# The last product of a gated attention and feed-forward kernel: scratch banks of two pieces, the order of the last two pieces, and a join of all columns

## The chip, the cores and the metric

The kernel runs on one core of a Trainium2 chip. The core has a matrix engine (TensorE, "PE" in the profile, with its weight loads as "PEld"), a vector engine (VectorE, "DVE"), a scalar engine (ScalarE, "ACT"), GpSimd ("POOL"), and a queue engine (SyncE, "SP") that here issues DMA transfers. Matrix products are accumulated in eight banks of 128 x 512 fp32 values, which DVE and ACT read. The metric is the device time of one execution in microseconds; less is better.

## The reference, cut to what matters

```
x = A_x                                    # 2048 rows, 1024 columns, bf16
g = sigmoid((x * gate_w).sum(-1))          # one number per row
a = attention(x, wqkv) @ wo                # 32 heads, 8 keys per query, 2 rows apart
h = gelu(x @ w_gate) * (x @ w_up)          # 3584 columns   (computed from B_x)
b = h @ w_down
return g * a + (1 - g) * b
```

The tail of the kernel, which this case is about, computes the two products with `wo` and `w_down` as one: the attention's output and h stand side by side as one long left operand, and `wo` and `w_down` one above the other as the right operand. The scale of the rows is applied when a finished sum leaves the banks.

## The kernel before, in words

The 2048 rows are cut into four chunks of 512. Most products are done by a scheme of the Strassen kind: two by two blocks, seven products instead of eight, with sums and differences of blocks ("forms") built by DVE. For the final product of a chunk (`down`, line 1635, and `down_rest`, line 1684) a block of 128 rows meets 18 tiles of 128 along the sum and 512 output columns. The seven products m = 0 to 6 each run for two pairs of row blocks, g = 0 and g = 1. In the last chunk product m = 5 is not done plainly for each g. `fifth` (line 1521) does both at once, by a second, inner scheme of the same kind: its left blocks are A(g, i), with i the even or odd tiles along the sum, its right blocks raw(i, j), with j the left or right half of the 512 columns (`lo` and `hi`, 256 each). Its forms are made well ahead by `fifth_rights` (line 1483) and `fifth_lefts` (line 1499).

The inner scheme has seven pieces, `o1` to `o7`, in the order of the code o1, o5, o6, o2, o7, o3, o4. Each is nine matmuls of 128 x 128 weights and 256 columns (`prod`, line 1540, matmul at line 1544). Three banks hold them:

- X is a scratch bank, taken by `bank_take` (line 267; of the free banks it gives the one that its last user leaves first). o1, o6 and o7 accumulate in its `lo` half, one on top of the other, and o5 stands in its `hi` half.
- Dk[0] holds an earlier product for g = 0; o2 adds to its `lo` half and o3 to its `hi` half.
- Dk[1] holds the same for g = 1; o4 adds to its `lo` half.

Beside each bank there is a fp32 buffer u2[g] (128 x 512) with a scaled product of before. `add` (line 1550, instruction at line 1552) scales a half of X by a number per row and adds it to a half of u2[g]. The adds are called a (after o1), b (two of them, after o5, one for each g), d (after o6) and f (two of them, after o7). `out` (line 1557, instruction at line 1562) scales a half of Dk[g], adds the half of u2[g] and writes the final bf16 half row; `evac` (line 1689, issue at line 1692) then has SP issue the store of that half to DRAM. There are four such joins: out(0, lo), out(1, hi), out(0, hi), out(1, lo).

The order of instructions on each engine is fixed when the program is built. A planner (`Weave`, line 44) walks through streams of operations that carry estimated costs and dependencies, and emits the one that can start first; every engine then runs its list in order. The stream of `fifth` is one generator, so its own operations come in the order of its `yield`s. The dependencies handed to `pe` and `dve` guide the planner. The waits that really go into the program are set from what each instruction reads and writes, and the buffers it shares with others.

Two instructions near the tail that the steps also use: line 1715, a join of the same form as line 1562 over all 512 columns, used for another product of the same chunk; and line 1700, ACT's scaled copy of a whole bank.

Of the kernel before, what the change touches and what calls it, by code (L numbers as in the profile page):

```python
# [155 lines left out]
def kernel(  # L156
# [12 lines left out]
    nc = tc.nc  # L169
# [21 lines left out]
    NW = D // 2  # L191
# [39 lines left out]
    banks = [psum.tile([P, SC], F32, name=f"ps{i}") for i in range(8)]  # L231
# [3 lines left out]
    w = Weave(nc, tc)  # L235
# [18 lines left out]
    def dve(cost, fn, deps=(), **kw):  # L254
        return Op("DVE", cost, fn, deps, **kw)
# [4 lines left out]
    def pe(n, fn, deps=(), **kw):  # L260
        return Op("PE", n * MM, fn, deps, tail=0.17, **kw)
# [5 lines left out]
    def bank_take(seeded=False, dirty=False):  # L267
        ok = [i for i in range(len(bank_free)) if not (seeded and bank_free[i][0] in partly)]
        if dirty:
            ok = [i for i in ok if bank_free[i][0] in partly] or ok  # L270
        best = min(ok, key=lambda i: -1.0 if bank_free[i][1] is None else bank_free[i][1].end)
        partly.discard(bank_free[best][0])
        return bank_free.pop(best)
# [1181 lines left out]
    lefts = [hT[:, 0:KP, NST - 1, :], hT[:, KP:2 * KP, 0, :], hT[:, KP:2 * KP, 1, :]]  # L1455

    def wide(q, k):
        if q < 8:
            return flat_of(lend[q // 4])[:, (q % 4 * 4 + k) * HW:(q % 4 * 4 + k + 1) * HW]
        return hrow[:, 20 + k // 2, k % 2 * HW:(k % 2 + 1) * HW]  # L1460

    def raw5(q, i, j):
        if q < 8:
            return flat_of(lend[4 + q // 4])[:, (q % 4 * 4 + 2 * i + j) * HW:(q % 4 * 4 + 2 * i + j + 1) * HW]
        return hrow[:, 18 + i, j * HW:(j + 1) * HW]
# [13 lines left out]
    def halves(c):  # L1479

        return {(g, i): [z.rearrange("p (q i) s -> p q i s", i=2)[:, :, i] for z in views(c)[g]["S4"]] for g in range(2) for i in range(2)}
# [39 lines left out]
    def fifth(c, Dk, u2, ops, omg, evac, ost_tile):  # L1521
        RT = {1: 0, 3: 1, 2: 2, 4: 3}
        S = halves(c)
        nh = FH // 2
        X, fr = bank_take()
        lo, hi = slice(0, HW), slice(HW, 2 * HW)

        def A(g, i):
            return lambda q: S[g, i][0][:, q] if q < nh else S[g, i][1][:, q - nh]

        def of(z):
            return lambda q: z[:, q]

        def raw(i, j):
            return lambda q: raw5(q, i, j)

        def T(f):
            return lambda q: wide(q, RT[f])

        def prod(bk, cols, lhs, rhs, start, deps):  # L1540
            for q0 in range(0, KP, 3):
                def fn(q0=q0):
                    for q in range(q0, q0 + 3):
                        nc.tensor.matmul(banks[bk][:, cols], lhsT=lhs(q), rhs=rhs(q), start=(start and q == 0),  # L1544
                                         stop=(q == KP - 1), skip_group_check=True)
                o = pe(1.515, fn, [x_ for x_ in deps if x_ is not None])
                yield o
            return o

        def add(g, cols, src, deps):  # L1550
            om = omg[:, 2 * g:2 * g + 1]
            return dve(0.42, lambda: nc.vector.scalar_tensor_tensor(out=u2[g][:, cols], in0=banks[X][:, src], scalar=om, in1=u2[g][:, cols],
                                                                    op0=ALU.mult, op1=ALU.add), deps)

        boxes = [[], []]

        def out(g, cols, deps):
            om = omg[:, 2 * g:2 * g + 1]

            def fn():  # L1560
                dst = boxes[g][0] if boxes[g] else ost_tile(boxes[g])
                nc.vector.scalar_tensor_tensor(out=dst[:, cols], in0=banks[Dk[g]][:, cols], scalar=om, in1=u2[g][:, cols],  # L1562
                                               op0=ALU.mult, op1=ALU.add)
            yield from evac(dve(0.42, fn, deps), 2 * g, 1, boxes[g], cols.start, cols.stop)
        rights = [("ir5", q) for q in range(KP)]
        raws = [("fw", q) for q in (0, 4, 7, 8)]
        j = {n: [("j%d" % n, k) for k in range(2)] for n in (1, 2, 3, 4)}
        m5 = [("inner", c)]
        o1 = yield from prod(X, lo, A(0, 0), raw(0, 0), True, [fr] + raws + [("S4", c, 0, 1)])
        a = add(0, lo, lo, [o1])  # L1570
        yield a
        o5 = yield from prod(X, hi, of(lefts[0]), T(1), False, rights + j[1])
        b = [add(g, hi, hi, [o5]) for g in range(2)]
        yield from b
        o6 = yield from prod(X, lo, of(lefts[1]), T(2), False, [a] + j[2])
        d = add(0, hi, lo, [o6])
        yield d
        o2 = yield from prod(Dk[0], lo, A(0, 1), raw(1, 0), False, m5)
        yield from out(0, lo, [o2, a])
        o7 = yield from prod(X, lo, A(1, 0), T(3), False, [d] + j[3])  # L1580
        f = [add(1, cols, lo, [o7]) for cols in (lo, hi)]
        yield from f
        o3 = yield from prod(Dk[0], hi, of(lefts[2]), raw(1, 1), False, j[4])
        yield from out(1, hi, [f[1], b[1]])
        yield from out(0, hi, [o3, d, b[0]])
        o4 = yield from prod(Dk[1], lo, A(1, 1), T(4), False, [])
        yield from out(1, lo, [o4, f[0]])
        w.done["pr", c, 5, 1] = o4

    def views(c):  # L1590
        cc = c % 2
# [92 lines left out]
    def down_rest(c, prod, ops, ev, A, Bk, Dk, m5, u2, omg, steps):  # L1684
# [35 lines left out]
        for m, g in steps:  # L1720
            if True:
# [17 lines left out]
                elif m == 3:  # L1739
                    o = yield from prod(Bk[g], m, g, False, [ev[g, "seed"]])  # L1740

                    def cp2(g=g, om1=om1):
                        u2[g] = work.tile([P, NW], F32, tag="u2", bufs=2, name="u2d")
                        scaled(Bk[g], om1, u2[g][:])
                    ev[g, "u2"] = act(0.6, cp2, [o])
                    yield ev[g, "u2"]
                elif m == 4:
                    ev[g, "m4"] = yield from prod(Bk[g], m, g, False, [ev[g, "u2"]], hooks=hk4 if g else hk3)
                    if g or c < INNER:
                        yield from joined(g)  # L1750
                elif m == 5 and c >= INNER:
                    yield from fifth(c, Dk, u2, ops, omg, evac, ost_tile)
                elif m == 5:
                    o = yield from prod(Dk[g], m, g, False, [ev[g, "m5"]])
                    e = dve(0.67, lambda g=g, om1=om1, box=box: nc.vector.scalar_tensor_tensor(
                        out=ost_tile(box), in0=banks[Dk[g]][:], scalar=om1, in1=u2[g][:], op0=ALU.mult, op1=ALU.add),
                        [o, ev[g, "u2"]])
                    yield from evac(e, j1, 1, box)
                    bank_give(Dk[g], e)
                else:  # L1760
                    o = yield from prod(Bk[g], m, g, False, [ev[g, "x"]])
                    e = act(0.6, lambda g=g, om2=om2, box=box: scaled(Bk[g], om2, ost_tile(box)), [o])
                    yield from evac(e, j2, 0, box)
                    bank_give(Bk[g], e)
# [58 lines left out]
```

## Time and profile before

| what | value |
|---|---|
| median of 3 timed runs | 717.35 us (717.07 to 718.23) |
| the profiled execution, its own time | 716.05 us |
| its span (first to last recorded event) | 714.3 us |
| PE busy | 704.8 us, 99% |
| DVE busy | 645.8 us, 90% |
| ACT busy | 328.9 us, 46% |
| POOL busy | 73.8 us, 10% |
| mean granted clock of PE | 0.999 |
| the pieces of `fifth`, first matmul to last | 701.58 to 711.2 us |
| last DVE instruction (line 1562) | 711.24 to 711.72 us |

The profile is of one execution. A timeline row gives the start, the duration, the engine, the line of the kernel, output <- inputs and the number of instructions merged in it; in brackets stands how long the engine had been idle before, and which instruction released it. The ends of matmuls are modelled, so gaps between matmuls are also read from start to start. Within the tail, "ps" is a bank, "u2d" the buffer u2, "ost" an output row block, "omg" the numbers per row, and "lend", "hT", "qo" hold blocks and forms.

### The profile page before, as it was taken

What the parts mean: (1) busy time and instruction counts of PE and PEld (TensorE: products, weight loads), DVE (VectorE), ACT (ScalarE), POOL (GpSimd) and SP (SyncE); (2) the same over time, 40 slices, a digit from 0 to 9 for tenths busy, and PEclk for the clock granted to TensorE, in tenths of its full rate; (3) what the DMA queues carried; (4) which work ended last, traced back from release to release, by engine and by line L of the source; (5) the groups of instructions that cost most, each with busy time, mean ns of one, the idle gap of its engine ahead of it and who ended that gap; (6) DMA issues with size and microseconds to landing.
All of it is one profiled execution on the core that took longest, in us unless ns stands there. A gap on an engine that the chain in (4) does not pass through costs nothing. (4 is left out here: it accounts for less than half of the span.)

```text
span 714.3 us, 10025 instructions
## 1 busy us (share of the span) xinstructions
PE 704.8 (99%) x3310; PEld 348.9 (49%) x3375; DVE 645.8 (90%) x963; ACT 328.9 (46%) x557; POOL 73.8 (10%) x130
## 2 busy tenths in 40 slices
PE   9999999999999999999999999999999999999997
PEld 5566544444444444456664444444444444444464
DVE  4999999999999999999689999899899999859782
ACT  5454685555665522153465313357655764221110
POOL 0040133433211000100000000100000000001000
PEclk9999999999999999999999999999999999999999
DMA  9963799996997799944459899996846574999980
GB/s 267 375 242 100 224 264 330 365 337 207 223 278 230 241 248 345 347 151 147 113 148 339 271 311 349 314 289 203 242 134 177 152 211 129 325 325 360 398 309 30
DMA packets 183477, 179.47 MB, mean 251 GB/s; under 512 B 56321, under 2 KB 139009, under 8 KB 183169
## 3 DMA queue, kind: packets, MB, share of 16 engines
q1 hardware_dynamic: 173808, 148.15, 70.0%
q0 software_dynamic: 9328, 30.42, 11.5%
q8 instruction: 26, 0.43, 0.2%
q10 hardware_dynamic: 288, 0.26, 0.1%
q14 instruction: 27, 0.21, 0.1%
HBM read 135.27 MB, written 31.46 MB: 233 GB/s over the span
## 5 line engine op out<-in xcount | busy, mean ns | idle before, releaser
L1241 PEld LDWEIGHTS <-ring 128*128 128x128 bf16 x1568 | 153.4, 98 | 184.9
L1241 PE MATMUL ps<-lend,ring 128*128 128x512 bf16 x878 | 210.9, 379 | 0.9
L1241 PE MATMUL ps<-tf,ring 128*128 128x512 bf16 x659 | 162.9, 379 | 0.7
L1659 PE MATMUL ps<-ring,hT 128*128 128x512 bf16 x665 | 153.5, 379 | 0.8
L1659 PEld LDWEIGHTS <-hT 128*128 128x128 bf16 x680 | 66.5, 98 | 79.8
L844 PEld LDWEIGHTS <-ring 128*128 128x128 bf16 x512 | 64.9, 127 | 45.8 <-DVE tf L533 0.4
L1189 DVE TENSOR_TENSOR xbuf<-xbuf,lend 128x2048 bf16<-128x2048 bf16 x64 | 77.9, 1221 | 3.0 <-DMA xbuf<-xbuf 2.8
L1042 DVE TENSOR_TENSOR xbuf<-qo,lend 128x2048 bf16<-128x2048 bf16 x64 | 77.2, 1219 | 0.0
L1048 DVE TENSOR_TENSOR xbuf<-xbuf 128x2048 bf16<-128x2048 bf16 x56 | 68.3, 1220 | 0.2
L844 PE MATMUL ps<-tf,ring 128*128 128x512 bf16 x251 | 57.8, 379 | 0.2
L844 PE MATMUL ps<-lend,ring 128*128 128x512 bf16 x250 | 57.5, 379 | 0.4
L1317 ACT ACTIVATE gl<-ps 128x512 bf16<-128x512 f32 x56 | 33.4, 597 | 48.1 <-PE ps L1241 46.9
L1273 ACT COPY ps<-ps 128x512 f32<-128x512 f32 x56 | 32.1, 573 | 50.7 <-PE ps L1241 50.5
L1692 POOL DMA_DIRECT2D out_dram<-ost x24 | 13.0, 541 | 338.0 <-ACT ost L1700 251.0
L1659 PE MATMUL ps<-ring,qo 128*128 128x512 bf16 x180 | 46.9, 379 | 0.2
L1700 ACT ACTIVATE ost<-ps,omg 128x512 bf16<-128x512 f32 x16 | 11.0, 687 | 78.1 <-PE ps L1659 74.9
L521 POOL DMA_DIRECT2D fforms<-ring x56 | 30.6, 546 | 127.0 <-DVE ring L512 114.0
L1290 DVE TENSOR_TENSOR hT<-hT,gl 128x1024 bf16<-128x1024 bf16 x56 | 38.4, 686 | 5.6 <-ACT hT L1283 5.4
L1329 DVE TENSOR_TENSOR u<-ps,u 128x512 f32<-128x512 f32 x56 | 38.5, 688 | 3.3 <-PE ps L1241 2.5
L1308 DVE TENSOR_TENSOR hT<-ps,m 128x512 bf16<-128x512 f32 x56 | 38.5, 687 | 2.4 <-PE ps L1241 2.2
L1325 ACT COPY u<-ps 128x512 f32<-128x512 f32 x56 | 32.8, 585 | 15.5 <-PE ps L1241 15.5
L1199 DVE TENSOR_TENSOR xbuf<-xbuf 128x2048 bf16<-128x2048 bf16 x32 | 39.1, 1221 | 0.1
(166 smaller groups left out, 728.5 us busy)
## 6 DMA issues: line engine op xcount, KB each, us to landing
ring<-dforms SPq DMA_DIRECT2D x105, 256.0 KB, 5.4
ring<-in_B_w_down_dram SPq DMA_DIRECT2D x77, 256.0 KB, 5.3
ring<-in_B_w_gate_dram SPq DMA_DIRECT2D x56, 256.0 KB, 5.5
fforms<-ring POOLq DMA_DIRECT2D x56, 256.0 KB, 5.4
ring<-fforms SPq DMA_DIRECT2D x56, 256.0 KB, 4.5
ring<-in_B_w_up_dram SPq DMA_DIRECT2D x42, 256.0 KB, 5.2
ring<-in_A_wqkv_dram SPq DMA_DIRECT2D x32, 256.0 KB, 4.5
ring<-oforms SPq DMA_DIRECT2D x30, 256.0 KB, 5.6
```

Of the source, the lines that this page charges most:

```text
L844: nc.tensor.matmul(banks[bk][:], lhsT=lhsT, rhs=rhs[:, kt, :], start=(start and kt == 0), stop=(kt == KH - 1), skip_group_check=True)
L1042: V(out=w3(box[t]), in0=q_b, in1=k_w, op=ALU.mult)
L1048: V(out=w3(box[0]), in0=w3(box[0]), in1=w3(box[t]), op=ALU.add)
L1189: return dve(tt(n), taking(("p", t), lambda: V(out=w3(box["p", t]), in0=w3(box["ab"]), in1=v_w, op=ALU.mult)), [("qkv", c, 2, t), abo] + ( ...
L1199: V(out=p0.rearrange("p (u n) -> p u n", u=2), in0=lo, in1=hi, op=ALU.add)
L1241: nc.tensor.matmul(banks[bk][:], lhsT=wv[:, k, fl * P:(fl + 1) * P], rhs=rhs[:, k, :], start=(start and k == 0), stop=(k == KH - 1), skip_ ...
L1290: yield dve(tt(2 * SC), lambda hv=hv, gv=gv: nc.vector.tensor_tensor(out=hv, in0=hv, in1=gv, op=ALU.mult), [e, ev[f, "g1"], ev[f, "g2"]], ...
L1308: ev[f, "up2"] = dve(tt(SC, True), lambda f=f: nc.vector.tensor_tensor(out=hs(f, 1), in0=v3(banks[Bk[f]][:]), in1=v3(m5[f][:]), op=ALU.add ...
L1317: nc.scalar.activation(out=gl[f][:, r1 * SC:(r1 + 1) * SC], in_=banks[A[f]][:], func=ACT.Gelu_apprx_tanh)
L1325: nc.scalar.copy(out=u2[f][:], in_=banks[Bk[f]][:])
L1329: e = dve(tt(SC, True), lambda f=f: nc.vector.tensor_tensor(out=u2[f][:], in0=banks[Dk[f]][:], in1=u2[f][:], op=ALU.add), [o, ev[f, "u2"]])
L1659: nc.tensor.matmul(banks[bk][:, o0:o0 + cols[1] - cols[0]], lhsT=l, rhs=wv[:, i, cols[0]:cols[1]], start=(start and k == 0), stop=(q == la ...
```

## The change

A second scratch bank Y is taken beside X. The piece o5 goes to the `lo` half of Y, as the first product of that bank, and its two adds b read Y. The other scratch pieces stay in X. The two last pieces change places: o4 now comes directly behind o7 and its adds f, and o3 is last. The two joins for g = 1 become one of all 512 columns behind o4, with one store of 128 KB; the join and store for g = 0, `hi`, are last. There are as many matmuls as before, of the same shapes; one DVE instruction and one store fewer.

```diff
         X, fr = bank_take()
+        Y, fy = bank_take()
...
-        def add(g, cols, src, deps):
+        def add(g, cols, bk, deps):
...
-            return dve(0.42, ... in0=banks[X][:, src], scalar=om, in1=u2[g][:, cols],
+            return dve(0.42, ... in0=banks[bk][:, lo], scalar=om, in1=u2[g][:, cols],
...
-            yield from evac(dve(0.42, fn, deps), 2 * g, 1, boxes[g], cols.start, cols.stop)
+            yield from evac(dve(0.67 if cols.stop - cols.start == NW else 0.42, fn, deps), 2 * g, 1, boxes[g], cols.start, cols.stop)
...
         o1 = yield from prod(X, lo, A(0, 0), raw(0, 0), True, [fr] + raws + [("S4", c, 0, 1)])
-        a = add(0, lo, lo, [o1])
+        a = add(0, lo, X, [o1])
         yield a
-        o5 = yield from prod(X, hi, of(lefts[0]), T(1), False, rights + j[1])
-        b = [add(g, hi, hi, [o5]) for g in range(2)]
+        o5 = yield from prod(Y, lo, of(lefts[0]), T(1), True, [fy] + rights + j[1])
+        b = [add(g, hi, Y, [o5]) for g in range(2)]
         yield from b
         o6 = yield from prod(X, lo, of(lefts[1]), T(2), False, [a] + j[2])
-        d = add(0, hi, lo, [o6])
+        d = add(0, hi, X, [o6])
         yield d
         o2 = yield from prod(Dk[0], lo, A(0, 1), raw(1, 0), False, m5)
         yield from out(0, lo, [o2, a])
         o7 = yield from prod(X, lo, A(1, 0), T(3), False, [d] + j[3])
-        f = [add(1, cols, lo, [o7]) for cols in (lo, hi)]
+        f = [add(1, cols, X, [o7]) for cols in (lo, hi)]
         yield from f
+        o4 = yield from prod(Dk[1], lo, A(1, 1), T(4), False, m5)
+        yield from out(1, slice(0, NW), [o4, b[1]] + f)
         o3 = yield from prod(Dk[0], hi, of(lefts[2]), raw(1, 1), False, j[4])
-        yield from out(1, hi, [f[1], b[1]])
         yield from out(0, hi, [o3, d, b[0]])
-        o4 = yield from prod(Dk[1], lo, A(1, 1), T(4), False, [])
-        yield from out(1, lo, [o4, f[0]])
-        w.done["pr", c, 5, 1] = o4
+        w.done["pr", c, 5, 1] = o3
```

More of the change, by code (lines that the diff above doesn't have):

```diff
@@ L1548, in prod @@
             return o
-        def add(g, cols, src, deps):
+        def add(g, cols, bk, deps):
             om = omg[:, 2 * g:2 * g + 1]
-            return dve(0.42, lambda: nc.vector.scalar_tensor_tensor(out=u2[g][:, cols], in0=banks[X][:, src], scalar=om, in1=u2[g][:, cols],
+            return dve(0.42, lambda: nc.vector.scalar_tensor_tensor(out=u2[g][:, cols], in0=banks[bk][:, lo], scalar=om, in1=u2[g][:, cols],
                                                                     op0=ALU.mult, op1=ALU.add), deps)
```

## The prediction

> **What bounds the kernel now.** I read the page first: TensorE (PE) is busy 704.8 us of the 714.3 us span, the granted clock is 0.999, and the chain of waits that ended last runs only through PE and the VectorE (DVE) combines of the last product. The diff touches nothing but that product, so I went to the last 14 us. There the waits view, for 700 to 716 us (columns: total us, times, longest), shows PE waiting for DVE three times:
>
> ```profile
> DVE u2d L1552 <- PE ps L1544: 9.7, 4, 6.8
> ...
> PEld L1544 <- issue: 2.6, 3, 1.1
> PE ps L1544 <- DVE u2d L1552: 1.5, 2, 1.0
> ...
> PE ps L1544 <- DVE ost L1562: 0.6, 1, 0.6
> ```
>
> Three holes, 1.5 + 0.6 = 2.1 us by modelled matmul ends, 2.6 us by the weight loads beside them. The timeline view (start, duration, engine, line, what; in brackets the idle time before it and its releaser) places them:
>
> ```profile
> 702.46 0.27 PE L1544 MATMUL ps<-hT,qo 128*128 128x256 bf16 x1
> ...
> 702.77 0.48 DVE L1552 SCALAR_TENSOR_TENSOR u2d<-ps,omg,u2d 128x256 f32<-128x256 f32 x1 [6.76 <-PE ps L1544]
> 703.30 1.03 PE L1544 MATMUL ps<-lend,hT 128*128 128x256 bf16 x8 [0.57 <-DVE u2d L1552]
> ...
> 704.17 0.27 PE L1544 MATMUL ps<-hT 128*128 128x256 bf16 x1
> 704.48 0.88 DVE L1552 SCALAR_TENSOR_TENSOR u2d<-ps,omg,u2d 128x256 f32<-128x256 f32 x2 [1.24 <-PE ps L1544]
> 705.41 1.03 PE L1544 MATMUL ps<-lend,hT 128*128 128x256 bf16 x8 [0.97 <-DVE u2d L1552]
> ...
> 706.28 0.27 PE L1544 MATMUL ps<-hT 128*128 128x256 bf16 x1
> 706.39 0.93 PE L1544 MATMUL ps<-lend,hT 128*128 128x256 bf16 x7
> ...
> 709.23 0.27 PE L1544 MATMUL ps<-hT 128*128 128x256 bf16 x1
> 709.53 0.88 DVE L1562 SCALAR_TENSOR_TENSOR ost<-ps,omg,u2d 128x256 bf16<-128x256 f32 x2
> 710.06 0.92 PE L1544 MATMUL ps<-lend,hT 128*128 128x256 bf16 x7 [0.56 <-DVE ost L1562]
> ...
> 710.93 0.27 PE L1544 MATMUL ps<-hT,qo 128*128 128x256 bf16 x1
> 711.24 0.48 DVE L1562 SCALAR_TENSOR_TENSOR ost<-ps,omg,u2d 128x256 bf16<-128x256 f32 x1 [0.84 <-PE ps L1544]
> ```
>
> The reader should see a strict alternation at the three holes: PE ends a piece, DVE reads the bank, and only then PE goes on. The listed dependencies do not ask for it: o5 (the piece of line 1572) does not list the add a, o6 (1575) lists a and not the adds b, o4 (1586) lists nothing. Each waits because it writes the other half of a bank that DVE is just reading. Between holes PE starts a matmul each 0.11 us (706.28 to 706.39); a piece of nine takes 0.98 us.
>
> **The change, part by part.** I count holes from start to start, less the 0.11 us pitch.
>
> (1) *o5 gets the bank Y.* Now o5 starts at 703.30, after the add a (ends 703.25); it could start at 702.46 + 0.11 = 702.57. Gain 0.73 us. In the changed program's list of instructions the first matmul of o5 carries no wait; its ninth carries one on DVE, for a right-hand form that the timeline shows done at 696.0, or at the latest for a, over at 703.25 when that matmul is due at 703.44. Cost nothing either way.
>
> (2) *o6 no longer waits for b.* Now it starts at 705.41, with the last matmul of o5 at 704.17: 705.41 - 704.28 = 1.13 us gone. What is late next: o6 still needs a. On the new clock o5 starts at 702.57, o6 is due at 703.55, and a ends at 703.25 plus 0.05 us (703.25 to 703.30 now). Cover 0.25 us; without it the excess would be paid.
>
> (3) *o4 goes ahead of o3, with one join of 512 columns.* Now o4 starts at 710.06 where 709.23 + 0.11 = 709.34 was possible: 0.72 us gone. o4's bank was last read by ScalarE, in the copy that started at 692.29, so its wait is long satisfied. A satisfied wait costs nothing that shows: o2's first matmul carries one on ScalarE already and starts 0.11 us after its predecessor (706.39). o3 writes a bank that the join out(0, lo) has read; that join moves to about 705.7 to 706.2, and o3 is due at 707.48.
>
> Sum for PE: 0.73 + 1.13 + 0.72 = **2.58 us**. The last matmul starts at 710.93 - 2.58 = 708.35 instead of 710.93.
>
> (4) *Does DVE keep up?* On the new clock: a 702.77 to 703.25; both b 703.75 to 704.63; d at 704.73 (o6's last matmul at 704.42 plus the 0.31 us between 710.93 and 711.24) to 705.21, and o7 needs d at 705.52 (cover 0.26 us after the 0.05); out(0, lo) 705.71 to 706.19; both f 706.69 to 707.57; o4's last matmul starts at 707.37, so the join can start at 707.68. It is dearer than a half: the same form at 512 columns (line 1715) took 0.75 us against 0.48. It ends at 708.43, and out(0, hi) is due at 708.35 + 0.31 = 708.66. Cover 0.23 us. The join carries six semaphore waits; line 1715 with five ran after two queue events of 50 and 154 ns, so I bound the added event between 0 and 0.15 us. That fits under the cover, and I take 0. For all of DVE: 0, bounds 0 to 0.25 us, as if the cover were overdrawn by its own size. No bound below nothing: the last instruction is the same 256-column form.
>
> (5) *Stores.* SP issues two instead of three after the halves: 128 KB after the join (issue at 708.47), 64 KB after the last (709.18). An issue occupies SP 0.33 to 0.38 us, so the second finds the queue free. After an engine's end at 702.47 the 128 KB store moved its data from about 703.33 to 703.9; shifted to 708.43 that is 709.3 to 709.9, while the last store's data starts 0.85 us after its combine's end (712.55 after 711.72 now), at 710.0. They just miss each other. I take 0, bounds 0 and 0.5 us (the whole transfer of the 128 KB). From the last combine to the span's end I keep 714.3 - 711.72 = 2.58 us, which only by chance is the same number.
>
> The Trainium skill, *DMA: Bandwidth & Descriptors*, section "Queues, rings and completion order", speaks against this tail: a completion signal lands only after every earlier write of the same DMA engine, so a large store just ahead can hold back the small one. By that rule the last store could not complete before the 128 KB one; the landings of the trace, 1.7 us for 128 KB and 1.6 us for 64 KB, give 710.2 and 710.8, so the sum stays as it is by the rule too.
>
> **Sum.** The profiled execution took 716.05 us, span 714.3; minus 2.58 gives 713.47, span 711.7. The median of the timed runs is 717.35, 1.30 us above the profiled one; the holes are in both, so I forecast **714.8 us**, 0.36% less. A measurement of this kernel can tell about 0.2%, 1.43 us, from no change (the three runs span 1.16).
>
> **The rivals.**
>
> *The holes shrink but do not all go.* The covers are 0.23 to 0.26 us. If DVE starts later than I have it by twice the cover, at a, d and the join, that returns some 0.75 us; with the last transfer queued, 0.5 more. That gives up to 1.25 us back: 714.8 to 716.0. For it: the covers are thin against waits of 0.05 us. Against: they come from one regular rhythm, and d to o7 has the same cover now (d ends 707.07, o7 starts 707.38 without a hole).
>
> *Nothing gained: the end is a transfer.* The join's store could land late. It decides the end from a landing of 714.3 - 0.94 - 708.47 = 4.9 us (0.94 being what follows the last landing now, 711.76 + 1.6 to 714.3). The first store of this chunk, at 690.37, did take 5.0 us, with 383 GB/s of loads around it. That would give 717.4. Against: the load traffic is over by 695.0, and all later stores landed in 1.6 to 1.7 us. By the rule of the Trainium skill named above this case would hold the last store as well; it adds no time. The same 717.4 comes out if the change does not do what it says and a wait on DVE reappears at each piece; the list of waits speaks against that.
>
> *Slower: PE loses clock.* Without holes PE runs the 54 matmuls from o5 on in one go, 54 x 0.109 = 5.9 us at full clock. The windows view shows that this core does grant half a clock, in the idle tail (columns: stretch, length, busy times of PE, PEld, DVE, ACT and POOL, PEclk, DMA share, GB/s):
>
> ```profile
> 712.60:712.90 0.30, 0.00 (x0) 0.00 (x0) 0.00 (x0) 0.00 (x0) 0.00 (x0) 0.84 0.73 212
> 712.90:713.20 0.30, 0.00 (x0) 0.00 (x0) 0.00 (x0) 0.00 (x0) 0.00 (x0) 0.50 0.01 2
> ```
>
> If dense work drew the same answer, 5.9 x (1/c - 1) would eat the gain from a clock of c = 0.70 down; at 0.50 it costs 5.9 us, and 714.8 + 5.9 = 720.7. Against: that reduction follows idleness, and in the windows from 694 to 702 us, with PE busy throughout, the clock is 1.00.
>
> **How the numbers follow.** Forecast 0.80, at 714.8 with its own range 714.0 to 715.6. Shrunk holes 0.10, up to 716.0, about 0.07 of it still over 0.2%. Nothing gained 0.07. Slower 0.03. So faster 0.80 + 0.07 = 0.87, same 0.03 + 0.07 = 0.10, slower 0.03. The range goes up to 716.0 (the first rival and all bounds of (4) and (5), 0.75 us, and a spread of runs on them) and down to 713.8, since the profiled execution shows that a run can lie 1.30 us under the median; that leaves out the last two rivals and a little of the spread.
>
> **What would show it.** In the changed kernel's timeline: 63 matmuls of the last product at one pitch, about 701.6 to 708.6, no idle entry on PE above 0.1 us, at o5, o6 and o4 each; one 128x512 combine of 0.75 us that starts near 707.7; the last combine at about 708.7, directly behind PE; two landings of 1.6 to 1.7 us; span 711.7. Wrong would be an idle entry on PE with a DVE releaser (steps 1 to 3), a last combine that follows DVE rather than PE (4), or more than 2.7 us from the last combine to the end (5). If all of that holds and the time does not move by 2 us or more, then the time outside the span, or some earlier part, moved the other way, and my premise that nothing ahead of the last product changes is wrong.

## The result and the profile after

| | before | after |
|---|---|---|
| timed runs, median | 717.07 us (715.95 to 718.23, 7 runs) | 714.59 us (713.38 to 715.37, 7 runs) |
| profiled execution, its own time | 716.05 us | 713.38 us |
| its span | 714.3 us | 711.6 us |
| first matmul of the last product to the end of the span ("the tail") | 701.58 to 714.3: 12.72 us | 701.42 to 711.6: 10.18 us |

The changed kernel is faster by 0.35%: ratio 0.9965, 95% interval 0.9952 to 0.9978, by the medians 2.48 us. The forecast was 714.8. Of the 2.7 us between the two spans, 2.54 us lie in the tail and 0.16 us in its earlier start.

The waits view of the changed kernel for 700 to 716 us (total us, times, longest) has three rows, of which two concern the last product:

```profile
DVE u2d L1553 <- PE ps L1545: 7.8, 3, 6.8
...
DVE ost L1563 <- PE ps L1545: 0.7, 2, 0.5
```

The reader is to see what is missing: no row in which PE waits for DVE is left, and the row of held-up weight loads (2.6 us) is gone too. In both rows that are left it is DVE that waits for PE. The timeline at the places of the three holes (start, duration, engine, line, what, idle time before and its releaser; the lines of the kernel moved down by one):

```profile
701.42 0.93 PE L1545 MATMUL ps<-lend,hT 128*128 128x256 bf16 x7
...
702.29 0.27 PE L1545 MATMUL ps<-hT,qo 128*128 128x256 bf16 x1
...
702.40 1.04 PE L1545 MATMUL ps<-lend,hT 128*128 128x256 bf16 x8
702.61 0.48 DVE L1553 SCALAR_TENSOR_TENSOR u2d<-ps,omg,u2d 128x256 f32<-128x256 f32 x1 [6.76 <-PE ps L1545]
703.28 0.27 PE L1545 MATMUL ps<-hT 128*128 128x256 bf16 x1
703.39 1.04 PE L1545 MATMUL ps<-lend,hT 128*128 128x256 bf16 x8
703.59 1.47 DVE L1553 SCALAR_TENSOR_TENSOR u2d<-ps,omg,u2d 128x256 f32<-128x256 f32 x3 [0.50 <-PE ps L1545]
...
706.22 0.27 PE L1545 MATMUL ps<-hT,qo 128*128 128x256 bf16 x1
...
706.33 0.93 PE L1545 MATMUL ps<-lend,hT 128*128 128x256 bf16 x7
...
707.21 0.27 PE L1545 MATMUL ps<-hT,qo 128*128 128x256 bf16 x1
...
707.32 1.04 PE L1545 MATMUL ps<-lend,hT 128*128 128x256 bf16 x8
707.60 0.75 DVE L1563 SCALAR_TENSOR_TENSOR ost<-ps,omg,u2d 128x512 bf16<-128x512 f32 x1 [0.19 <-PE ps L1545]
708.19 0.27 PE L1545 MATMUL ps<-hT 128*128 128x256 bf16 x1
708.50 0.48 DVE L1563 SCALAR_TENSOR_TENSOR ost<-ps,omg,u2d 128x256 bf16<-128x256 f32 x1
```

At 702.40 o5 starts 0.11 us behind o1 and runs beside the add a; at 703.39 o6 starts 0.11 us behind o5, beside b; at 706.33 o4 starts 0.11 us behind o7, beside the adds f; at 707.32 o3 starts 0.11 us behind o4, beside the wide join. The last combine starts at 708.50, 0.31 us behind the start of the last matmul, so PE and not DVE sets it.

### The profile page after: what moved, and what is told of

The parts are those of the page before. It is cut to its first block, busy times and chain, and to the rows that moved or that the text cites. A ratio compares the mean times of both kernels' runs of the same rounds, so it can differ in the third digit from the quotient of the medians.

```text
span 711.6 us, 10088 instructions
## 1 busy us (share of the span) xinstructions
PE 707.3 (99%) x3375; PEld 348.7 (49%) x3375; DVE 645.5 (91%) x962; ACT 329.1 (46%) x557; POOL 74.0 (10%) x130
## 4 chain that ended last, share of the span: by engine, by line
PE 97%; DMA 2%; SPq 0%; DVE 0%; issue 0%
PE ps L1241 48%; PE ps L1659 28%; PE ps L844 19%; DMA lend<-in_A_x_dram 1%; PE ps L613 1%; PE ps L1545 1%; PE ps L1412 1%; DMA hT<-in_A_x_dram 1%; SPq L442 0%; DVE tf L533 0%; PE ps L946 0%; DVE ost L1563 0%; PE ps L1003 0%
```

## The experiments

The theory: PE lost 2.58 us because three pieces write a bank that DVE is just reading, in other columns; each hole is 0.31 us (last matmul's start to DVE's start), plus the DVE work up to the end of its read of that bank, plus 0.05 us back to PE, less the pitch of 0.11 us, and less what PE does meanwhile. The main rival: the gain comes from the new order and the wide join, that is from one instruction and one store less. I judge by the tail, since its start alone differs by up to 2.9 us between the traces below (701.42 to 704.34). Spans are printed to 0.1 us, so a tail is known to about 0.05. The starts of the first and the last matmul of the last product are printed to 0.01 us, so the stretch between them shows the holes alone, without the stores; it has a column of its own. The two parts (bank only, order and join only) were timed in 11 runs each, the kernel before beside them in 21; each of the other variants ran once, and for them only the trace counts.

| kernel | tail starts | span | first to last matmul, us | tail, us | tail expected |
|---|---|---|---|---|---|
| before | 701.58 | 714.3 | 9.35 | 12.72 | |
| as changed | 701.42 | 711.6 | 6.77 | 10.18 | 10.14 (12.72 - 2.58) |
| bank only | 703.06 | 713.9 | 7.49 | 10.84 | 10.86 |
| order and join only | 703.12 | 715.2 | 8.63 | 12.08 | 12.00 |
| join in halves | 702.05 | 712.2 | 6.77 | 10.15 | 10.2 to 10.3 |
| half of the join ahead of o4 | 701.42 | 713.2 | 8.47 | 11.78 | 11.9 |
| o7 ahead of o2 | 702.37 | 713.5 | 7.51 | 11.13 | 11.15 |
| no store of the join | 701.59 | 711.8 | 6.77 | 10.21 | 10.18 |
| last store from two queues | 704.34 | 715.1 | 6.77 | 10.76 | 10.0 to 10.1, or 10.2, or more |
| last store in halves from SP | 701.44 | 712.5 | 6.77 | 11.06 | 11.0 or more, or 10.5 or less |
| last store from ScalarE | 702.13 | 712.4 | 6.77 | 10.27 | 10.2, or 10.4 to 10.8 |

### The bank alone

```diff
 (from the changed kernel: Y kept, order and joins as before)
-        o4 = yield from prod(Dk[1], lo, A(1, 1), T(4), False, m5)
-        yield from out(1, slice(0, NW), [o4, b[1]] + f)
         o3 = yield from prod(Dk[0], hi, of(lefts[2]), raw(1, 1), False, j[4])
+        yield from out(1, hi, [f[1], b[1]])
         yield from out(0, hi, [o3, d, b[0]])
+        o4 = yield from prod(Dk[1], lo, A(1, 1), T(4), False, [])
+        yield from out(1, lo, [o4, f[0]])
```

> The bank Y alone, with the order and the joins of before. I measure the tail from the first matmul of the last product to the end of the span: 12.72 us before, 10.18 after. Theory of the shared bank: the holes ahead of o5 and o6 go (0.73 and 1.13 us), the one ahead of o4 stays at 0.72, tail 10.86. Rival, that the order and the one join bring the gain by having less for DVE and the queue to do: the tail stays near 12.7. In time, by the theory, 1.86 us less than before.

The tail is 10.84 us, and the time is 0.9978 of the kernel before (interval 0.9968 to 0.9988, or 0.9 to 2.3 us less; the expected 1.86 lies in it). In the waits view one pair of rows on the last product's PE is left:

```profile
PEld L1545 <- issue: 0.7, 1, 0.7
PE ps L1545 <- DVE ost L1563: 0.6, 1, 0.6
```

That is the hole ahead of o4, unchanged; the two at o5 and o6 are gone without any change of order. The rival of the order would have left the tail near 12.7.

### The order and the wide join alone

```diff
 (from the kernel before: X for both halves kept)
-        o3 ...; out(1, hi); out(0, hi); o4 ...; out(1, lo)
+        o4 = yield from prod(Dk[1], lo, A(1, 1), T(4), False, m5)
+        yield from out(1, slice(0, NW), [o4, b[1]] + f)
+        o3 = yield from prod(Dk[0], hi, of(lefts[2]), raw(1, 1), False, j[4])
+        yield from out(0, hi, [o3, d, b[0]])
```

> The new order and the one join of 512 columns, with o5 back in the upper half of X. Theory of the shared bank: holes of 0.73 and 1.13 us ahead of o5 and o6, none ahead of o4 and o3, tail 12.72 - 0.72 = 12.00. Rival of the order: tail near 10.2. The two parts together, if they add up, give 1.86 + 0.72 = 2.58 us.

The tail is 12.08 us; the time ratio is 0.9990 (0.9980 to 1.0000), so by time alone this part is not clear of nothing. The waits of PE on the adds are all there, and the one on the join is not:

```profile
PEld L1544 <- issue: 1.9, 2, 1.1
PE ps L1544 <- DVE u2d L1552: 1.5, 2, 1.0
```

So the parts are worth 1.88 and 0.64 us by the tail, together 2.52 us against 2.54 for both at once. From first to last matmul they are worth 9.35 - 7.49 = 1.86 and 9.35 - 8.63 = 0.72 us, together 2.58, and both at once 9.35 - 6.77 = 2.58: they add up, each has the size that was expected, and nearly three quarters of the gain is the bank's.

### The join in two halves

```diff
-        yield from out(1, slice(0, NW), [o4, b[1]] + f)
+        yield from out(1, lo, [o4, f[0]])
+        yield from out(1, hi, [f[1], b[1]])
```

> As changed, but the join of g = 1 in two instructions and two stores of 256 columns, both behind o4. Theory: DVE ends the second half some 1.27 us after the start of o4's last matmul, the last combine is due 1.29 us after it, so it costs 0 to 0.1 us: tail 10.2 to 10.3. Rival, that the wide join itself (one instruction, one store less) is a part of the gain: 0.4 us or more back, tail 10.6.

The tail is 10.15 us, as with the wide join. Its timeline:

```profile
708.20 1.41 DVE L1563 SCALAR_TENSOR_TENSOR ost<-ps,omg,u2d 128x256 bf16<-128x256 f32 x3 [0.16 <-PE ps L1545]
708.82 0.27 PE L1545 MATMUL ps<-hT 128*128 128x256 bf16 x1
```

The two halves and the last combine run in one chain of 1.41 us that ends at 709.61; with PE as the setter it would end at 708.82 + 0.31 + 0.48 = 709.61. So PE sets it. Two halves back to back take 0.88 us (as the adds f do), so the second half ended at 709.08, 0.05 us before the last combine started at 709.13. The width of the join, and the instruction and store it saves, are worth nothing here that the trace shows.

### Half of the join ahead of o4

```diff
+        yield from out(1, hi, [f[1], b[1]])
         o4 = yield from prod(Dk[1], lo, A(1, 1), T(4), False, m5)
-        yield from out(1, slice(0, NW), [o4, b[1]] + f)
+        yield from out(1, lo, [o4, f[0]])
```

> As changed, with o4 ahead of o3, but the join of g = 1 split, its upper half ahead of o4 as it was before. Theory: o4 writes the bank that this half reads, so it waits from o7's last matmul for 0.31 us, both adds f (0.88), 0.09, the half join (0.48) and 0.05, less the pitch of 0.11: a hole of 1.70 us, tail 11.9, longer than with the old order of the pieces. Rival, that the change of places of o3 and o4 is what frees PE: no hole, tail 10.2.

```profile
706.22 0.27 PE L1545 MATMUL ps<-hT,qo 128*128 128x256 bf16 x1
706.54 0.88 DVE L1553 SCALAR_TENSOR_TENSOR u2d<-ps,omg,u2d 128x256 f32<-128x256 f32 x2 [0.50 <-PE ps L1545]
707.50 0.48 DVE L1563 SCALAR_TENSOR_TENSOR ost<-ps,omg,u2d 128x256 bf16<-128x256 f32 x1
708.04 0.92 PE L1545 MATMUL ps<-lend,hT 128*128 128x256 bf16 x7 [1.54 <-DVE ost L1563]
```

The timeline shows the chain itself: adds f, half join, and only then o4, 708.04 - 706.22 - 0.11 = 1.71 us late (1.70 expected). The tail is 11.78 us, 0.1 less than expected; that difference lies behind the last combine (710.68 to 713.2, 2.52 us against 2.62 in the changed kernel). With the places changed but a read of o4's bank ahead of it, the new order is worse than the old one with Y (10.84), where o3 covered part of the chain. What frees PE is that every read of Dk[1] stands behind o4.

### o7 ahead of o2

```diff
-        o2 ...; out(0, lo, ...); o7 ...
+        o7 ...; o2 ...; out(0, lo, ...)
```

> As changed, with o7 ahead of o2, so that o7 meets the add d on the bank X with no piece between them. Theory of the shared bank: o7 waits 0.31 + 0.48 + 0.05 - 0.11 = 0.73 us. With the order of the code the adds f then come behind out(0, lo), so DVE is late by about 0.24 us at the last combine: tail 10.18 + 0.97 = 11.15. Theory with the cover of DVE left out: 10.91. Rival, that PE's waits on DVE come from the number of waits and not from a piece too few between them: 10.2.

```profile
705.21 0.27 PE L1545 MATMUL ps<-hT 128*128 128x256 bf16 x1
706.06 0.93 PE L1545 MATMUL ps<-lend,hT 128*128 128x256 bf16 x7 [0.57 <-DVE u2d L1553]
...
709.68 1.14 DVE L1563 SCALAR_TENSOR_TENSOR ost<-ps,omg,u2d 128x512 bf16<-128x512 f32 x2 [0.19 <-issue]
709.88 0.27 PE L1545 MATMUL ps<-hT 128*128 128x256 bf16 x1
```

The hole is 706.06 - 705.21 - 0.11 = 0.74 us (0.73 expected). DVE's pair starting at 709.68 ends at 710.82, where PE alone would have allowed 709.88 + 0.79 = 710.67: late by 0.15 us, somewhat less than the 0.24 of the working. The pair took 1.14 us, not 0.75 + 0.48 = 1.23: the second of two DVE instructions back to back starts 0.09 us before the first one's end, and 0.09 is the difference. The tail is 11.13 us, between the version with DVE's lateness (11.15) and the one without (10.91), and next to the first. A hole can be made at will, in its computed size, by taking away the piece between.

### The store of the join left out

```diff
+            if cols.stop - cols.start == NW:
+                yield dve(0.67, fn, deps)
+                return
```

> As changed, with the store of the join of 512 columns left out (so this part of the output is not written). Theory: the 128 KB ahead of the last store cost it nothing, since their data ends at 709.75 and the last data begins at 709.95: from the last combine's end to the span's end 2.6 us as now (2.62). Rival, a completion that waits for the bigger store ahead of it: 2.1 to 2.4 us.

The last combine ends at 707.77 + 1.38 = 709.15 and the span at 711.8: 2.65 us, against 2.62 in the changed kernel (708.98 to 711.6). The 128 KB ahead of the last store cost it nothing. The windows view of the changed kernel suggests why (the last two columns are the DMA engines' share and GB/s):

```profile
709.30:709.60 0.30, 0.00 (x0) 0.00 (x0) 0.00 (x0) 0.00 (x0) 0.00 (x0) 1.00 1.00 341
709.60:709.90 0.30, 0.00 (x0) 0.00 (x0) 0.00 (x0) 0.00 (x0) 0.00 (x0) 1.00 0.20 60
709.90:710.20 0.30, 0.00 (x0) 0.00 (x0) 0.00 (x0) 0.00 (x0) 0.00 (x0) 1.00 0.64 186
```

There is a trough between the two transfers: they do not meet. What a meeting would cost was not tried.

### The last store: two queues, one queue in halves, another queue

These three look for a version with a shorter end. Each changes only how the last 64 KB store is issued; the edits are given in words.

```
as changed:  one store of 128 rows by SP
first:       rows 0-63 by SP, rows 64-127 by ScalarE
second:      rows 0-63 by SP, then rows 64-127 by SP
third:       all 128 rows by ScalarE
```

> As changed, with the last 64 KB store in two halves of 64 rows, one issued by SP and one by ScalarE. If the issue (0.33 us) and the transfer (0.25 us) of the rows are on the path, 0.1 to 0.25 us less from the last combine to the end: 2.4 to 2.5 us. If the landing is a fixed 1.6 us whatever the size: 2.6 us as now. If ScalarE issues later than SP: more than 2.6.

It came out worse: from the last combine's end (711.90) to the end of the span (715.1) 3.2 us, not 2.6. Both issues took 0.57 us and the halves landed after 1.9 and 2.1 us, not 1.6. More than 2.6 us had been expected only if ScalarE issued later than SP; it did not (711.94 against 711.93), so the reason given for that case was not the one at work. Its own time, 716.86 us, even lies above the 715.99 of the kernel before on the same chip, though its tail is 1.96 us shorter: the tail simply started late in that execution.

> As changed, with the last 64 KB store in two halves of 64 rows, both issued by SP, one after the other. With two queues at once each issue took 0.57 us, not 0.33, and the time from the last combine's end to the span's end was 3.2 us, not 2.6. If a store of 64 rows is dear by itself: two issues of 0.57 us, end 3.4 us or more after the combine. If two issues at once were in each other's way: each 0.33 us or less, end 2.6 + 0.33 = 2.95 us or less.

> As changed, with the last 64 KB store whole, but issued by ScalarE alone. If ScalarE's queue is the slower one: an issue well over 0.33 us and 2.8 to 3.2 us from the last combine's end to the end of the span. If the two issues at once were the trouble: 0.33 us and 2.6 us, as with SP.

In halves from SP the end is 3.5 us behind the combine (709.00 to 712.5); whole from ScalarE 2.7 us (709.69 to 712.4). The rows of the stores, one from each kernel (duration of an issue in ns, least, middle, most), for the changed kernel, the halves from SP and the whole from ScalarE:

```profile
L1692 SPq DMA_DIRECT2D out_dram<-ost x7: 332/332/338, 690.1 to 709.0; - x7
```

```profile
L1571 SPq DMA_DIRECT2D out_dram<-ost x2: 562/572/582, 709.0 to 709.6; - x2
```

```profile
L1571 ACTq DMA_DIRECT2D out_dram<-ost x1: 378/378/378, 709.7 to 709.7; - x1
```

A store of 64 rows is the dear one, on either queue and also when only one queue issues: 0.57 us to issue against 0.33 for 128 rows. The explanation by two issues in each other's way falls. The whole store from ScalarE lies between its two expectations: 0.38 us to issue is more than the 0.33 on SP, but the end of 2.7 us is nearer to 2.6 than to 2.8 to 3.2. None of the versions beats the changed kernel.

## Why the prediction was right

(1) and (2), o5 and o6: the sum had 0.73 + 1.13 = 1.86 us; the bank alone gave 1.88 by the tail and 1.86 from first to last matmul. The shared bank, not the dependencies listed in the code, was the cause. The Trainium skill, *PSUM — Partial Sum Buffer*, section "PSUM bank collisions raise a hardware error", says why a program has to wait here: two engines must be kept apart by bank and group of 32 partitions, even where they touch different columns (the pieces here use all 128 partitions). The traces show a kernel that does wait so: o5 waited 0.73 us for a read of the other half of its bank, and 0 us once it had a bank to itself. What would happen without the wait no run here shows.

(3), o4: 0.72 us in the sum, 0.64 by the tail of the order alone, and 0.72 from first to last matmul. The missing 0.08 of the tail is not a hole: that tail ends 2.66 us behind its last combine (711.16 + 1.38 = 712.54 to 715.2), where the kernel before has 2.58. The experiment with half a join ahead sharpens the reason: the change of places would have done harm by itself.

(4), DVE keeps up: the cover at the last combine was given as 0.23 us. The join started at 707.60, 0.08 us later than 707.21 + 0.31, inside the 0 to 0.15 us bounded for its added waits. It ended at 708.35, so 0.15 us of cover were left, counted as in the sum. That count is cautious by the 0.09 us that two DVE instructions back to back overlap. The experiments that use up the cover go the way computed: halves leave 0.05 us of it, o7 ahead of o2 overdraws it by 0.15 us.

(5), the stores: 0 was taken of 0 to 0.5 us, and leaving the big store out changed nothing (2.65 against 2.62 us). The time from last combine to the end was kept at 2.58 and is 2.62; this 0.04 us is the whole difference between 2.58 and the measured 2.54, and it is no more than the rounding of the spans. The start of the last store's data was put 0.85 us behind its combine's end; the rows given for it, 711.72 and 712.55, say 0.83, which changes nothing.

The rivals: shrunk holes did not occur, a late landing did not occur (1.7 us for the join's store), and the clock stayed at 1.00 through all 63 matmuls. The half clock of the idle end, on which the last rival rested, came at no fixed distance: it set in between 712.6 and 712.9 us in the kernel before (0.84 in that window), at most 2.0 us behind the last matmul's start, while in the changed kernel the clock was still 1.00 from 708.7 to 711.6, up to 3.4 us behind it. That it follows idleness is what one tail suggested, not a rule shown here. The step from span to median was luck in part: the median lay 1.21 us above the profiled execution where 1.30 was taken, but the runs spread over 1.99 us (changed) and 2.28 us (before), and over all seven runs the kernel before has 717.07, not the 717.35 of the first three.

## What to carry to other kernels

Look for a strict alternation in the timeline, matrix engine, reader, matrix engine, on the same bank; where the code lists no such dependency, the bank is shared, and its price can be computed from four rows: start of the last matmul to the reader's start, the reader's work, the way back, less the pitch. It goes if the piece gets a free bank, or if another piece of at least that length stands between; a change of order helps only if no read of the next bank is left ahead of it. Judge such a change by the stretch that it touches: here a single run's time could not have ranked the variants, the tail did to 0.1 us, and the stretch from first to last matmul came out at 6.77 us in all six kernels without a hole.

## What the runs showed that I had not expected

A store of 64 rows x 512 bytes took longer to issue (0.56 to 0.58 us in all four cases) than one of 128 rows x 512 or 1024 bytes (0.33 to 0.34 us on SP in the changed kernel, 0.38 on ScalarE), and landed later (1.9 to 2.1 us against 1.6). What in the 64 rows makes it dear was not tried. Between executions the tail started anywhere from 701.42 to 704.34 us, with the same program ahead of it but for line numbers. Between the changed kernel and the version with two queues, the two ends of that range, 0.8 us arise before the first matmul of line 844 (14.9 and 15.7 us) and 2.1 us between the first matmul of line 1241 (81.6 and 82.4) and the first of `down` (248.2 and 251.1). In that stretch PE of the changed kernel waits for nobody, and PE of the other waits once for DVE (1.0 us, line 1308) and once for ScalarE (0.4 us, line 1299). What brings these waits about was not tried.
